# Opening of a fused recurrence and maxout kernel: larger first blocks, longer weight rows, casts after the loads, more transposes by DMA

## The chip, the cores and the metric

The kernel runs on one core of a Trainium2 chip. The core has a matrix engine (TensorE, PE), a vector engine (VectorE, DVE), a scalar engine (ScalarE, ACT), a general engine (GpSimd, POOL) and SyncE (SP), which issues DMAs. Each works through its own instructions in order and waits on semaphores for the others. The metric is the device time of one run in microseconds, lower is better.

## The reference

```python
def _attn_ref(x, f_logit, lower_bound):       # x, f_logit: 4 x 6144 x 256
    sig = 1.0 / (1.0 + np.exp(-f_logit))
    f = lower_bound + (1.0 - lower_bound) * sig
    i = 1.0 - f
    for t in range(S):
        h = f[:, t] * h + i[:, t] * x[:, t]
        y[:, t] = h
    return y

def _moe_ref(x, w1, w2, w_out):               # x = y as 24576 x 256, d_ff = 1024
    h1 = x @ w1
    h2 = x @ w2
    g = np.maximum(h1, h2)
    return g @ w_out
```

A gated recurrence runs along time, separately for each of 256 channels and 4 sequences. Its output goes through two layers: the maximum of two products, and a product with `w_out`. Inputs and output are float32.

## The kernel before

**What is computed how.** The maximum is rewritten: max(h1, h2) = h1 + relu(h2 - h1). The first layer therefore multiplies by one matrix, `wd` (w2 minus w1, scaled), and ACT takes the ReLU of it out of PSUM as `rt`. The second layer adds `rt @ wob` (`wob` is w_out in bfloat16) to `y @ w13`, where `w13` is w1 times w_out, made once in the opening. A factor of one minus the lower bound is folded into the weights (`om`).

**Blocks and chunks.** Tokens are cut into blocks of at most 512 (`TB`) and chunks of at most 1024 (`CH`). A chunk is the unit that is fetched, a block the unit that is computed. The first sequence begins with chunks of 256, 256 and 512 tokens, one block each; every other chunk has 1024 tokens and two blocks. There are 26 chunks and 49 blocks.

**Getting channels onto partitions.** The recurrence wants channels on partitions and time along the row; memory has tokens in rows of 1 KB. There are three ways (`fetch`, `cross`, `turn_steps`):

- Chunk 0 is loaded as float32 by SP, and PE transposes it.
- Other chunks that are not `by_xbar` are cast to bfloat16 in a DMA that POOL issues, into a tile `fn` or `xn`; PE transposes 128 x 128 pieces of it into PSUM (`tT`), which ACT and DVE read there.
- Chunks that are `by_xbar` are cast by a POOL DMA into a scratch buffer in device memory (six for f, six for x, used in turn), and a transposing DMA that SP issues (`cross`) brings them into `fT` or `xT`. A scratch buffer is written again only after its transposing DMA has landed. `by_xbar` holds for f from chunk 5 on, and for x from chunk 5 on except chunks 7, 11, 15, 19 and 23.

**One block.** `gate` is a sigmoid on ACT, giving `u`. `scan_steps` are five DVE steps: `drive` (u times x), two `decay` and two `scan`, giving `y`. `first_layer(j, fc)` is two matmuls of 512 columns and one ReLU; there are eight per block. `second_layer(j, slot)` is an eighth of the block's 40 matmuls of 256 columns, with two copies out of PSUM and one output DMA per block on SP.

**Order.** All instructions stand in an order written by hand (`manual_schedule`). In the opening the weights come in four column groups of 256 (rows of 1 KB); w1 is scaled on ACT (`make_w1s`), `wd` is made on DVE (`make_wd`), w1 is transposed on PE (`make_w1T`), and its product with `wob` gives `w13`. These steps are interleaved with the first three blocks. Then the loop runs over j: the first layer of block j, the second layer of block j-1, the transposes of block j+2, the scans of block j+1, and the gate of block j+2 after the middle of the block. `ahead` issues the casting DMAs 10 blocks early (`LEAD_FETCH`) and the transposing DMAs 5 blocks early (`LEAD_CROSS`). POOL does nothing but DMAs after its first instructions, so its casts run as far ahead as buffers and its queue allow, whatever the loop has reached.

Of the kernel before, what the change touches and what calls it, by code (L numbers as in the profile page):

```python
# [9 lines left out]
FP32 = mybir.dt.float32  # L10
# [8 lines left out]
def kernel(  # L19
# [71 lines left out]
    def fetch(c):  # L91
        b, t0, nt, _ = chunks[c]
        for s in range(2):
            src = srcs[s][b, t0 : t0 + nt, :]
            if c == 0:
                nat = const.tile([P, nt // P, D], FP32, name=("f0", "x0")[s])
                nc.sync.dma_start(
                    out=nat[:], in_=src.rearrange("(i p) d -> p i d", p=P)
                )
                held[c, s] = nat  # L100
            elif by_xbar(c, s):
                scr = scratch[s][uses[s] % NSCR]
                uses[s] += 1
                nc.gpsimd.dma_start(  # L104
                    out=scr[0:nt, :].rearrange("(p i) d -> p (i d)", p=P),
                    in_=src.rearrange("(p i) d -> p (i d)", p=P),
                )
# [19 lines left out]
    def turn_steps(j):  # L127
        b, t0, nb, c, o = blocks[j]
        steps = []
        for s in range(2):  # L130
            if by_xbar(c, s):
                turned[j, s] = held[c, s][:, :, o : o + nb]
                continue
            if c == 0:
                dst = ps_t.tile([P, KC, nb], FP32, name="tT")
            else:
                dst = ps_t.tile([P, KC, TB], BF16, name="tT")
            turned[j, s] = dst[:, :, 0:nb]
            for q in range(nb // P):
                for h in range(KC):  # L140
                    steps.append(
                        (
                            dst[:, h, q * P : (q + 1) * P],
                            held[c, s][:, o // P + q, h * P : (h + 1) * P],
                        )
                    )
        return steps

    def turn(steps):
        for dst, src in steps:  # L150
            nc.tensor.transpose(dst, src, ident[:] if src.dtype == BF16 else ident_f[:])  # L151

    ys = {}

# [2 lines left out]
    def gate(j):  # L157
        nb = blocks[j][2]
        u = midpool.tile([P, KC, TB], BF16, name="u")
        nc.scalar.activation(  # L160
            out=u[:, :, 0:nb], in_=turned[j, 0], func=AF.Sigmoid, scale=-1.0
        )
        us[j] = u

    def scan_steps(j):
        b, t0, nb, c, o = blocks[j]
# [14 lines left out]
            )  # L181

        def drive():
            nc.vector.tensor_tensor(  # L184
                out=v[:, :, 0:nb], in0=u[:, :, 0:nb], in1=turned[j, 1], op=ALU.mult
            )

        def scan(h):
# [22 lines left out]
    def recurrence(j):  # L211
        gate(j)
        for step in scan_steps(j):
            step()
# [1 line left out]
    ident_f = const.tile([P, P], FP32)  # L216
    make_identity(nc, ident_f[:])
    ident = const.tile([P, P], BF16)
    nc.vector.tensor_copy(out=ident[:], in_=ident_f[:])
    om = const.tile([P, KC], FP32)  # L220
    nom = const.tile([P, KC], FP32)
    lbc = const.tile([P, KC], FP32)
    warm = const.tile([P, 1], FP32)
    nc.sync.dma_start(out=lbc[:], in_=lower_bound.rearrange("(h p) -> p h", p=P))
    nc.vector.tensor_scalar(
        out=om[:], in0=lbc[:], scalar1=-1.0, scalar2=1.0, op0=ALU.mult, op1=ALU.add
    )
    nc.vector.tensor_scalar_add(out=nom[:], in0=lbc[:], scalar1=-1.0)

    w1n = wpool.tile([P, KC, DFF], FP32)  # L230
    w2n = wpool.tile([P, KC, DFF], FP32)
# [7 lines left out]
    def gcols(g):  # L239
        return slice(g * DFF // NG, (g + 1) * DFF // NG)  # L240

    def fetch_w(g):
        for w, src in ((w2n, moe_w2), (w1n, moe_w1)):
            nc.sync.dma_start(
                out=w[:, :, gcols(g)],
                in_=src[:, gcols(g)].rearrange("(kc p) f -> p kc f", p=P),
            )

    def make_w1s(g):
        for kc in range(KC):  # L250
            nc.scalar.mul(  # L251
                w1s[:, kc, gcols(g)], w1n[:, kc, gcols(g)], om[:, kc : kc + 1]
            )

    def make_wd(g):
        for kc in range(KC):
            nc.vector.scalar_tensor_tensor(  # L257
                out=wd[:, kc, gcols(g)],
                in0=w2n[:, kc, gcols(g)],
                scalar=om[:, kc : kc + 1],  # L260
                in1=w1s[:, kc, gcols(g)],
                op0=ALU.mult,
                op1=ALU.subtract,
            )

    def make_w1T(g):
        n = FC // NG
        pt = ps_o.tile([P, KC, n, P], FP32, name="psO")
        for kc in range(KC):
            for q in range(n):  # L270
                fc = n * g + q
# [3 lines left out]
        dst = w1T[:, n * g : n * g + n, :].rearrange("p q (k d) -> p k q d", k=KC)  # L275
        if g % 2:
            nc.scalar.copy(out=dst, in_=pt[:])
        else:
            nc.vector.tensor_copy(out=dst, in_=pt[:])

    def make_w13():
        for kc in range(KC):
# [84 lines left out]
    with tc.manual_schedule():  # L367
        fetch(0)
        fetch(1)
        for g in range(NG):  # L370
            fetch_w(g)
        nc.gpsimd.dma_start(
            out=wob[:], in_=moe_w_out.rearrange("(fc p) c -> p fc c", p=P)
        )
# [12 lines left out]
        turn(turn_steps(1))  # L387
        make_wd(1)
        recurrence(1)
        first_layer(0, 2)  # L390
        first_layer(0, 3)
        make_w1s(2)
        make_wd(2)
        make_w1T(0)
        make_w1T(1)
        first_layer(0, 4)
        first_layer(0, 5)
        make_w1s(3)
        make_wd(3)
        make_w1T(2)  # L400
        first_layer(0, 6)
        first_layer(0, 7)
        make_w1T(3)
        turn(turn_steps(2))
        gate(2)
        make_w13()
        done["fetch"] = 3
        ahead("fetch", fetch, LEAD_FETCH)
        ahead("cross", cross, LEAD_CROSS)
        for j in range(1, NBLK + 1):  # L410
            ahead("fetch", fetch, j + LEAD_FETCH)
            ahead("cross", cross, j + LEAD_CROSS)
            steps = turn_steps(j + 2) if j + 2 < NBLK else []
            scans = scan_steps(j + 1) if j + 1 < NBLK else []
# [40 lines left out]
```

## Time and profile before

| | |
|---|---|
| median of 3 runs | 418.28 us (418.23 to 418.82) |
| the profiled execution: time of the run | 418.23 us |
| its span, first to last instruction | 415.8 us |
| PE busy, DVE busy, ACT busy, POOL busy | 95%, 58%, 66%, 7% |
| read from device memory, written to it | 53.48 MB, 44.56 MB |
| mean granted TensorE clock | 0.992 |

Times in the profile count from the start of the span. A row of the timeline gives the start, the duration, the engine, the line of the kernel, the operation, the tile written and the tile read, and in square brackets the idle time before it and what ended that. A row of groups gives the sum of busy time and the mean duration of one in nanoseconds. A row of the windows gives the stretch, its length, the busy time of each engine, the granted clock, the busy share of the DMA engines and GB/s written. A row of DMA issues ends with the time from issue to landing. Matmuls are pipelined, so that the rate of several in a row is read from their starts.

### The profile page before, as it was taken

What the parts mean: (1) busy time and instruction counts of PE and PEld (TensorE: products, weight loads), DVE (VectorE), ACT (ScalarE), POOL (GpSimd) and SP (SyncE); (2) the same over time, 40 slices, a digit from 0 to 9 for tenths busy, and PEclk for the clock granted to TensorE, in tenths of its full rate; (3) what the DMA queues carried; (4) which work ended last, traced back from release to release, by engine and by line L of the source; (5) the groups of instructions that cost most, each with busy time, mean ns of one, the idle gap of its engine ahead of it and who ended that gap; (6) DMA issues with size and microseconds to landing.
All of it is one profiled execution on the core that took longest, in us unless ns stands there. A gap on an engine that the chain in (4) does not pass through costs nothing.

```text
span 415.8 us, 7247 instructions
## 1 busy us (share of the span) xinstructions
PE 395.5 (95%) x2872; PEld 304.8 (73%) x2920; DVE 239.3 (58%) x354; ACT 274.1 (66%) x457; POOL 30.9 (7%) x57
## 2 busy tenths in 40 slices
PE   2699997999999999999999999999999999999996
PEld 2487774777777777777777777777777777777775
DVE  2545563665665764665665566566476575566641
ACT  2667655766766766776776676676676676677662
POOL 8122001000001000010010010000000000000000
PEclk9989998999999999999999999999999999999999
DMA  8998989999799999999999999872852453811212
GB/s 192 233 232 199 223 178 230 261 240 110 135 196 217 268 249 122 237 207 173 245 251 192 184 224 251 202 177 89 192 123 82 151 112 92 203 52 50 99 54 102
DMA packets 100657, 73.09 MB, mean 176 GB/s; under 512 B 79040, under 2 KB 93888, under 8 KB 100032
## 3 DMA queue, kind: packets, MB, share of 16 engines
q1 hardware_dynamic: 87152, 46.93, 49.4%
q0 software_dynamic: 13184, 25.43, 37.6%
q8 instruction: 23, 0.38, 0.3%
q10 hardware_dynamic: 288, 0.26, 0.2%
q14 instruction: 10, 0.08, 0.1%
HBM read 53.48 MB, written 44.56 MB: 236 GB/s over the span
## 4 chain that ended last, share of the span: by engine, by line
PE 83%; DMA 15%; issue 1%; ACT 0%; POOL 0%; DVE 0%; POOLq 0%; ACTq 0%
PE psO L330 48%; PE dT L301 34%; DMA fT<-scr_0_90 7%; DMA scr_0_90<-in_f_logit_dram 6%; DMA xn<-in_x_dram 2%; PE tT L151 1%; ACT u L160 0%; POOL fn L111 0%; ACT rt L309 0%; DVE osb L339 0%; POOL ident_f masks.py:199 0%; POOL ident_f masks.py:197 0%; POOLq masks.py:199 0%; ACTq L160 0%; POOLq L439 0%
## 5 line engine op out<-in xcount | busy, mean ns | idle before, releaser
L309 ACT ACTIVATE rt<-dT 128x512 bf16<-128x512 f32 (+1 forms) x392 | 225.7, 587 | 117.8 <-PE dT L301 115.7
L330 PE MATMUL psO<-wob,rt 128*128 128x256 bf16 x1536 | 230.8, 273 | 2.3
L301 PE MATMUL dT<-y,wd 128*128 128x512 bf16 (+1 forms) x736 | 221.6, 378 | 10.1 <-DVE wd L257 7.0
L330 PEld LDWEIGHTS <-rt 128*128 128x128 bf16 x1536 | 169.6, 113 | 42.9 <-issue 0.6
L350 DVE COPY osb<-psO 128x512 f32<-128x512 f32 x94 | 65.0, 692 | 153.0 <-PE psO L330 153.0
L194 DVE TENSOR_TENSOR_SCAN y<-ff,y,v 128x512 bf16<-128x512 bf16 (+1 forms) x90 | 109.2, 1255 | 0.0
L301 PEld LDWEIGHTS <-wd 128*128 128x128 bf16 x784 | 71.9, 98 | 16.9 <-DVE wd L257 9.5
L330 PE MATMUL psO<-w_122,y 128*128 128x256 bf16 x384 | 73.7, 273 | 0.3
L330 PEld LDWEIGHTS <-y 128*128 128x128 bf16 x384 | 43.3, 113 | 41.6 <-issue 0.6
L160 ACT ACTIVATE u<-fT 128x1024 bf16<-128x1024 bf16 x42 | 44.0, 1048 | 4.0 <-DMA fT<-scr_0_90 4.0
L174 DVE TENSOR_SCALAR ff<-u,nom 128x512 bf16<-128x512 bf16 (+1 forms) x98 | 29.7, 347 | 0.0
L151 PE MATMUL tT<-ident,xn 128*128 128x128 bf16 x124 | 23.6, 228 | 0.0
L184 DVE TENSOR_TENSOR v<-u,xT 128x1024 bf16<-128x1024 bf16 x32 | 21.8, 681 | 2.2 <-DMA xT<-scr_0_96 2.2
L184 DVE TENSOR_TENSOR v<-u,tT 128x1024 bf16<-128x1024 bf16 (+1 forms) x17 | 11.3, 664 | 7.6 <-PE tT L151 4.0
L151 PEld LDWEIGHTS <-xn 128*128 128x128 bf16 x124 | 12.3, 103 | 0.3
L251 ACT ACTIVATE w1s<-w1n,om 128x256 f32<-128x256 f32 x8 | 3.6, 500 | 7.1 <-DMA w1n<-in_moe_w_dram 7.1
L194 DVE TENSOR_TENSOR_SCAN y<-ff,v 128x512 bf16<-128x512 bf16 (+1 forms) x8 | 8.3, 1074 | 0.0
L111 POOL DMA_DIRECT2D xn<-in_x_dram x9 | 7.9, 883 | 2.3 <-DMA xn<-in_x_dram 2.2
L160 ACT ACTIVATE u<-tT 128x1024 bf16<-128x1024 bf16 (+2 forms) x7 | 6.3, 898 | 2.1 <-PE tT L151 2.1
L257 DVE SCALAR_TENSOR_TENSOR wd<-w2n,om,w1s 128x256 bf16<-128x256 f32 x8 | 3.5, 479 | 4.5 <-ACT w1s L251 4.5
L151 PE MATMUL tT<-ident,fn 128*128 128x128 bf16 x44 | 6.1, 245 | 0.0
L104 POOL DMA_DIRECT2D scr_0_90<-in_f_logit_dram x4 | 2.0, 500 | 49.5 <-DMA fT<-scr_0_90 49.0
(40 smaller groups left out, 49.0 us busy)
## 6 DMA issues: line engine op xcount, KB each, us to landing
out_dram<-osb SPq DMA_DIRECT2D x46, 512.0 KB, 3.8
xn<-in_x_dram POOLq DMA_DIRECT2D x7, 512.0 KB, 15.0
scr_0_90<-in_f_logit_dram POOLq DMA_DIRECT2D x4, 512.0 KB, 9.0
scr_1_91<-in_f_logit_dram POOLq DMA_DIRECT2D x4, 512.0 KB, 7.3
scr_2_92<-in_f_logit_dram POOLq DMA_DIRECT2D x4, 512.0 KB, 14.1
scr_0_96<-in_x_dram POOLq DMA_DIRECT2D x3, 512.0 KB, 19.9
scr_1_97<-in_x_dram POOLq DMA_DIRECT2D x3, 512.0 KB, 9.9
scr_3_93<-in_f_logit_dram POOLq DMA_DIRECT2D x3, 512.0 KB, 8.6
```

The lines of the kernel that those rows point to most:

```text
L111: nc.gpsimd.dma_start(out=nat[:, 0 : nt // P, :], in_=src.rearrange("(i p) d -> p i d", p=P),)
L151: nc.tensor.transpose(dst, src, ident[:] if src.dtype == BF16 else ident_f[:])
L160: nc.scalar.activation(out=u[:, :, 0:nb], in_=turned[j, 0], func=AF.Sigmoid, scale=-1.0)
L174: nc.vector.tensor_scalar(out=ff[:, h, 0:nb], in0=u[:, h, 0:nb], scalar1=nom[:, h : h + 1], scalar2=1.0, op0=ALU.mult, op1=ALU.add,)
L184: nc.vector.tensor_tensor(out=v[:, :, 0:nb], in0=u[:, :, 0:nb], in1=turned[j, 1], op=ALU.mult)
L194: nc.vector.tensor_tensor_scan(out=y[:, h, 0:nb], data0=ff[:, h, 0:nb], data1=v[:, h, 0:nb], initial=init, op0=ALU.mult, op1=ALU.add,)
L251: nc.scalar.mul(w1s[:, kc, gcols(g)], w1n[:, kc, gcols(g)], om[:, kc : kc + 1])
L257: nc.vector.scalar_tensor_tensor(out=wd[:, kc, gcols(g)], in0=w2n[:, kc, gcols(g)], scalar=om[:, kc : kc + 1], in1=w1s[:, kc, gcols(g)], o ...
L301: nc.tensor.matmul(dT[:, 0:nb], lhsT=wd[:, kc, fc * P : (fc + 1) * P], rhs=y[:, kc, 0:nb], start=(kc == 0), stop=(kc == KC - 1),)
L309: nc.scalar.activation(out=rt[:, 0:nb], in_=dT[:, 0:nb], func=AF.Relu)
L330: nc.tensor.matmul(ps[:, r, :], lhsT=left, rhs=right, start=(s == 0 and (r == 0 or j == NBLK - 1)), stop=(s == n - 1 and (r == 1 or j == N ...
L350: nc.vector.tensor_copy(out=osb[:, 2 * g : 2 * g + 2, :], in_=ps[:])
```

## The change

- The first sequence begins with four chunks of 512 tokens (one block each) instead of 256, 256 and 512. There are 26 chunks and 48 blocks.
- Chunk 0 comes with four tokens, 4 KB, per partition and is cast to bfloat16 by DVE. The other chunks that PE transposes come with four tokens per partition as well. After the transposes the tokens of a block stand permuted in PSUM; the gate and the drive read PSUM with a stride of 128 elements to undo that (`like`).
- The weights w1 and w2 come in two column halves, rows of 2 KB; `w_out` comes in rows of 4 KB. Hidden units are permuted to suit, the same in `wd`, `w1T` and `wob`.
- POOL issues the cast of `w_out` only after the first half of w1 has landed, and all other casts only after the second half of w2 has landed (`pool_waits`).
- From chunk 6 on all of x goes by transposing DMA (`by_xbar`); chunk 5 of x is now transposed by PE.
- Transposing DMAs are issued 3 blocks early instead of 5. The gate of a block that came by transposing DMA moves from the middle of iteration j-2 to the start of iteration j-1.
- The opening finishes all eight first-layer slices of block 0 and `w13` before block 1 is turned; the loop starts at j = 2.

The core of the diff:

```diff
-        sizes = [256, 256, 512] if b == 0 else []
+        sizes = [TB] * 4 if b == 0 else []
...
-        return c >= 5 and (s == 0 or c % 4 != 3)
+        return c >= (5, 6)[s]
...
-                    out=nat[:], in_=src.rearrange("(i p) d -> p i d", p=P)
-                )
+                    out=raw[:], in_=src.rearrange("(p i) d -> p i d", p=P)
+                )
+                nat = natpool.tile([P, CH // P, D], BF16, name=("fn", "xn")[s])
+                nc.vector.tensor_copy(out=nat[:, 0 : nt // P, :], in_=raw[:])
...
-                    out=nat[:, 0 : nt // P, :],
-                    in_=src.rearrange("(i p) d -> p i d", p=P),
+                    out=nat[:, 0 : nt // P, :].rearrange(
+                        "p (k i) d -> p k (i d)", i=TB // P
+                    ),
+                    in_=src.rearrange(
+                        "(k p i) d -> p k (i d)", p=P, i=TB // P
+                    ),
...
+            turned[j, s] = dst[:, :, 0:nb].rearrange("p k (i m) -> p k m i", i=ns)
...
+        src = turned[j, 0]
         nc.scalar.activation(
-            out=u[:, :, 0:nb], in_=turned[j, 0], func=AF.Sigmoid, scale=-1.0
+            out=like(u[:, :, 0:nb], src), in_=src, func=AF.Sigmoid, scale=-1.0
         )
...
+    def like(t, src):
+        if len(src.shape) == 3:
+            return t
+        return t.rearrange("p k (m i) -> p k m i", m=P)
...
-    NG = 4
+    NG = 2
+    NQ = FC // NG
+    w1n = [wpool.tile([P, KC, NQ * P], FP32, name=f"w1n{g}") for g in range(NG)]
+    w2n = [wpool.tile([P, KC, NQ * P], FP32, name=f"w2n{g}") for g in range(NG)]
+
+    def half(w, g):
+        return w[g][:].rearrange("p kc (m q) -> p kc q m", q=NQ)
+
+    def fcs(w, kc, g):
+        return w[:, kc, g * NQ * P : (g + 1) * NQ * P].rearrange(
+            "p (q m) -> p q m", q=NQ
+        )
...
+    def pool_waits(t):
+        nc.gpsimd.tensor_copy(out=waited[:], in_=t)
...
-        if g % 2:
-            nc.scalar.copy(out=dst, in_=pt[:])
-        else:
-            nc.vector.tensor_copy(out=dst, in_=pt[:])
+        dst = w1T[:, 2 * k : 2 * k + 2, :].rearrange("p q (k d) -> p k q d", k=KC)
+        nc.scalar.copy(out=dst, in_=pt[:])
...
-    LEAD_CROSS = 5
+    LEAD_CROSS = 3
...
         fetch(0)
-        fetch(1)
         for g in range(NG):
             fetch_w(g)
-        nc.gpsimd.dma_start(
-            out=wob[:], in_=moe_w_out.rearrange("(fc p) c -> p fc c", p=P)
-        )
-        fetch(2)
...
         recurrence(0)
         make_w1s(0)
         make_w1s(1)
+        pool_waits(w1n[0][:, 0, 0:1])
+        nc.gpsimd.dma_start(
+            out=wob[:].rearrange("p (g q) c -> p g (q c)", g=NG),
+            in_=moe_w_out.rearrange("(g p q) c -> p g (q c)", g=NG, q=NQ),
+        )
+        pool_waits(w2n[1][:, 0, 0:1])
         make_wd(0)
-        first_layer(0, 0)
-        first_layer(0, 1)
-        turn(turn_steps(1))
+        for fc in range(0, NQ):
+            first_layer(0, fc)
+        fetch(1)
+        fetch(2)
+        done["fetch"] = 3
+        ahead("fetch", fetch, LEAD_FETCH)
         make_wd(1)
...
         make_w1T(0)
         make_w1T(1)
...
+        for fc in range(NQ, FC):
+            first_layer(0, fc)
         make_w1T(2)
...
         make_w1T(3)
+        make_w13()
+        turn(turn_steps(1))
+        recurrence(1)
+        for fc in range(FC):
+            second_layer(0, fc)
         turn(turn_steps(2))
-        gate(2)
-        make_w13()
-        done["fetch"] = 3
-        ahead("fetch", fetch, LEAD_FETCH)
-        ahead("cross", cross, LEAD_CROSS)
-        for j in range(1, NBLK + 1):
+        recurrence(2)
+        for fc in range(FC):
+            first_layer(1, fc)
+        turn(turn_steps(3))
+        gate(3)
+        for j in range(2, NBLK + 1):
...
+            gates = {}
+            if j + 1 < NBLK and by_xbar(blocks[j + 1][3], 0):
+                gates[0] = j + 1
+            if j + 2 < NBLK and not by_xbar(blocks[j + 2][3], 0):
+                gates[FC // 2] = j + 2
...
+                if fc in gates:
+                    gate(gates[fc])
+                if fc == 0 and j + 1 < NBLK:
+                    scans = scan_steps(j + 1)
                 if fc < len(scans):
                     scans[fc]()
-                if fc == FC // 2 and j + 2 < NBLK:
-                    gate(j + 2)
```

More of the change, by code (lines that the diff above doesn't have):

```diff
@@ L133, in turn_steps @@
                 continue
-            if c == 0:
-                dst = ps_t.tile([P, KC, nb], FP32, name="tT")
-            else:
-                dst = ps_t.tile([P, KC, TB], BF16, name="tT")
-            turned[j, s] = dst[:, :, 0:nb]
-            for q in range(nb // P):
+            dst = ps_t.tile([P, KC, TB], BF16, name="tT")
+            ns = nb // P
+            turned[j, s] = dst[:, :, 0:nb].rearrange("p k (i m) -> p k m i", i=ns)
+            for q in range(ns):
                 for h in range(KC):
@@ L150, in turn @@
         for dst, src in steps:
-            nc.tensor.transpose(dst, src, ident[:] if src.dtype == BF16 else ident_f[:])
+            nc.tensor.transpose(dst, src, ident[:])
     ys = {}
@@ L222 @@
     lbc = const.tile([P, KC], FP32)
+    waited = const.tile([P, 1], FP32)
     warm = const.tile([P, 1], FP32)
-    nc.sync.dma_start(out=lbc[:], in_=lower_bound.rearrange("(h p) -> p h", p=P))
-    nc.vector.tensor_scalar(
-        out=om[:], in0=lbc[:], scalar1=-1.0, scalar2=1.0, op0=ALU.mult, op1=ALU.add
-    )
-    nc.vector.tensor_scalar_add(out=nom[:], in0=lbc[:], scalar1=-1.0)
-    w1n = wpool.tile([P, KC, DFF], FP32)
-    w2n = wpool.tile([P, KC, DFF], FP32)
     wob = wpool.tile([P, FC, D], BF16)
@@ L250, in make_w1s @@
         for kc in range(KC):
[L251 to L253 removed]
+            nc.scalar.mul(fcs(w1s, kc, g), half(w1n, g)[:, kc], om[:, kc : kc + 1])
+    def pool_waits(t):
+        nc.gpsimd.tensor_copy(out=waited[:], in_=t)
     def make_wd(g):
@@ L257, in make_wd @@
             nc.vector.scalar_tensor_tensor(
-                out=wd[:, kc, gcols(g)],
-                in0=w2n[:, kc, gcols(g)],
+                out=fcs(wd, kc, g),
+                in0=half(w2n, g)[:, kc],
                 scalar=om[:, kc : kc + 1],
-                in1=w1s[:, kc, gcols(g)],
+                in1=fcs(w1s, kc, g),
                 op0=ALU.mult,
@@ L264, in make_wd, with make_w1T @@
             )
-    def make_w1T(g):
-        n = FC // NG
-        pt = ps_o.tile([P, KC, n, P], FP32, name="psO")
+    def make_w1T(k):
+        pt = ps_o.tile([P, KC, 2, P], FP32, name="psO")
         for kc in range(KC):
-            for q in range(n):
-                fc = n * g + q
+            for q in range(2):
+                fc = 2 * k + q
                 nc.tensor.transpose(
```

37 lines of the change are left out of this document (15 added, 22 removed).

## The prediction

> **What bounds the kernel now.** I read the page's first and fourth parts, then the chain in order of time, then the timeline of the opening and of the one hole, then the groups by form, then the DMA answers.
>
> ```profile
> span 415.8 us, 7247 instructions
> PE 395.5 (95%) x2872; PEld 304.8 (73%) x2920; DVE 239.3 (58%) x354; ACT 274.1 (66%) x457; POOL 30.9 (7%) x57
> 139.75 0.71 PE psO L330 x5
> 147.57 0.71 PE psO L330 x5
> 155.44 0.71 PE psO L330 x5
> 163.71 0.71 PE psO L330 x5
> 171.92 0.71 PE psO L330 x5
> 179.74 0.71 PE psO L330 x5
> 37.41 0.15 PEld L301 LDWEIGHTS <-wd 128*128 128x128 bf16 x2
> 407.69 0.22 PEld L330 LDWEIGHTS <-y 128*128 128x128 bf16 x2
> ```
>
> The span is 415.8 us and the profiled run took 418.23, so 2.4 us lie outside the span; the median of the runs is 418.28, practically the same. TensorE (PE) is busy 95% of it. The five-matmul pieces come once per block of 512 tokens: 7.82 us apart (139.75 to 147.57; 171.92 to 179.74) where PE only multiplies. Around 155 to 172 the three steps sum to 24.35 instead of 23.46: there PE also turned the x of one 1024-token chunk, 16 transposes, 0.89 us, or 0.056 each. From 37.41, where the third whole block's iteration starts (j=3), to 407.69, where only the last second layer is left, are 370.28 us for 46 iterations. At 7.82 that is 359.7; 10.6 us are extra. The other losses are the opening (37.4 us) and a tail of 8.1 us that the change leaves alone. The extra has a hole in it:
>
> ```profile
> 62.61 0.10 PEld L301 LDWEIGHTS <-wd 128*128 128x128 bf16 x1
> 64.12 1.06 ACT L160 ACTIVATE u<-fT 128x1024 bf16<-128x1024 bf16 x1 [4.02 <-DMA fT<-scr_0_90]
> 65.71 1.01 PE L301 MATMUL dT<-y,wd 128*128 128x512 bf16 x2 [2.83 <-ACT rt L309]
> 65.00:68.50 3.50, 2.79 (x10) 1.34 (x10) 1.22 (x3) 2.23 (x5) 0.94 (x2) 0.51 1.57 386
> ```
>
> ScalarE (ACT) waited 4.02 us for the first chunk turned by DMA, its ReLUs stood behind that wait, PE starved for 2.83 us, and then ran 3.5 us at a granted clock of 0.51, which is another 1.7. Together 4.4 to 4.5 us. Transposes make up the rest of the 10.6: 112 after 37.41, 6.2 us.
>
> **The change, part by part.** *Transposes in the loop.* From the point equal to 37.41 (in the new kernel the start of j=2, since its blocks 0 and 1 cover the old 0 to 2) 48 are left: f and x of chunk 4, x of chunk 5. 48 x 0.056 = 2.7 us against 6.2: **3.5 us gained**, on PE's path, as PE never waits there. What replaces them are four more DMA transposes, weighed below.
>
> *The opening.* The rows that price it:
>
> ```profile
> 10.05 0.91 ACT L251 ACTIVATE w1s<-w1n,om 128x256 f32<-128x256 f32 x2 [4.18 <-DMA w1n<-in_moe_w_dram]
> 13.18 0.91 ACT L251 ACTIVATE w1s<-w1n,om 128x256 f32<-128x256 f32 x2 [2.23 <-DMA w1n<-in_moe_w_dram]
> 4.00:5.00 1.00, 1.00 (x8) 0.83 (x6) 0.00 (x0) 0.00 (x0) 1.00 (x3) 1.00 1.20 265
> 20.00:25.00 5.00, 4.45 (x33) 3.98 (x34) 1.87 (x4) 2.63 (x5) 0.97 (x2) 0.66 1.45 198
> 22.30 1.06 PE L151 MATMUL tT<-ident,fn 128*128 128x128 bf16 x8
> 23.46 1.02 ACT L160 ACTIVATE u<-tT 128x1024 bf16<-128x1024 bf16 x1 [0.32 <-PE tT L151]
> 24.01 1.97 PE L285 MATMUL psO<-wob,w1T 128*128 128x256 bf16 x16
> 25.11 0.61 DVE L174 TENSOR_SCALAR ff<-u,nom 128x512 bf16<-128x512 bf16 x2
> 25.64 2.45 DVE L194 TENSOR_TENSOR_SCAN y<-ff,y,v 128x512 bf16<-128x512 bf16 x2
> L309 ACT ACTIVATE rt<-dT 128x512 bf16<-128x512 f32 x376 | 220.0, 596 | 115.0 <-PE dT L301 113.0 <-PE psO L330 1.5
> L257 DVE SCALAR_TENSOR_TENSOR wd<-w2n,om,w1s 128x256 bf16<-128x256 f32 x8 | 3.5, 479 | 4.5 <-ACT w1s L251 4.5
> L184 DVE TENSOR_TENSOR v<-u,tT 128x1024 bf16<-128x1024 bf16 x15 | 10.2, 678 | 3.1 <-ACT u L160 3.1
> L279 DVE CAST w1T<-psO 128x512 bf16<-128x512 f32 x2 | 1.4, 684 | 0.0
> 407.41 4.93 PE psO L330 x45
> ```
>
> Without casts beside it SP's queue gets six tiles of 512 KB: f0, x0, and two halves of each of w2 and w1. No row shows that queue alone. Below, it got 512 KB in 3.13 us beside casts (10.05 to 13.18, 168 GB/s); above, casts alone wrote 198 GB/s, which is 396 read. Nearest is the second from 4.0, mostly this queue: 265 written and, with casts read at twice their size, about 310 read. I take 310: 1.7 us a tile from 2.4 us (f0's first packets), 0.4 for the landing: f0 4.5, x0 6.2, w1's first half 9.6, its second 13.4 with some of w_out beside it.
>
> The casts of f0 and x0 are new on VectorE (DVE): 1024 elements, above 1.37 (twice the 684 ns of 512 from PSUM), below 0.61 (two decays, 1024 elements of bf16 from SBUF); I take 0.8, nearer the second, as it reads no PSUM. The drive now reads PSUM with a stride: between 0.68 as it stands and 1.37; I take 1.37. The sigmoid I leave at 1.02, for ACT takes elements one at a time in every row; were the stride to double it, each of three blocks in the opening would pay 1 us. Then y of block 0 is at 6.2 + 0.8 + 1.06 + 1.37 + 0.61 + 2.45 = 12.5, and two wd pieces of 512 (0.75 each, between one and two of 479) make 14.0. But ACT holds w1s of the second half (2 x 0.75, from 13.4) ahead of block 0's ReLUs: 14.9. From there ACT is the chain: 8 ReLUs of 0.59 and 4 copies of w1's transposes of 0.59 (two of these came from DVE) end at 22.0; the last 10 of w13's 16 matmuls (1.97 for all) 23.2; 16 transposes 1.8; second layer of block 0, 40 matmuls at 0.11 (45 in 4.93), 29.4; meanwhile gate, drive, decays and scans give y of block 1 at 29.6. 16 transposes, 31.2; the next 8 ReLUs pace the first layer, PE done 34.7; 16 transposes, 36.5. These transposes are at the half clock of that row (0.66 mean from 20 to 25); at 0.056 each the same sum gives 35.0. I take 36.0 for the start of j=2, **1.4 us earlier** than 37.41. PE there has done the same matmuls, so nothing is owed later. POOL's two waits delay only casts: the chunk 1 that block 1 needs at 23 is queued from about 11 behind w_out, 2 MB read at 396 GB/s, 17. The wait costs nothing there; its cost would be at the far end of the casts.
>
> *The hole.* Its price depends on those casts:
>
> ```profile
> 38.70 0.51 POOL L104 DMA_DIRECT2D scr_5_95<-in_f_logit_dram  x1 [2.10 <-DMA scr_1_91<-in_f_logit_dram]
> 41.29 0.49 POOL L104 DMA_DIRECT2D scr_4_100<-in_x_dram  x1 [2.08 <-DMA scr_1_97<-in_x_dram]
> scr_4_100<-in_x_dram POOLq DMA_DIRECT2D x1, 512.0 KB, 21.8
> fT<-scr_0_90 SPq DMA_TRANSPOSE x1, 30.7
> q0 software_dynamic: 128, 2.10, 97.7%
> q1 hardware_dynamic: 129, 0.03, 2.0%
> ```
>
> Casts run ahead without pause until their six scratch buffers are full, one 1024-token tile each 2.6 us; the last landed at 41.29 + 21.8 = 63.1. The transposing DMA issued at 33.33 took 30.7 us, to 64.0: it all but stood still until the casts were over. The last two rows (50 to 60 us) say why: both queues moved the same number of packets, the casts' 16 KB each on average, the others 0.2 KB. In the new kernel the casts queue w_out (2.6), six half tiles (7.8) and 14 whole ones up to chunk 10 (37.1) from about 10.7, plus 1.2 beside w1 and 2.6 for two outputs: over at 62.0. The first fT, now issued only after block 1's output at about 45, then lands near 63.3. Its gate is now at the start of j=5: 36.0 + 3 x 7.82 + 2.2 of transposes = 61.7. With three PSUM buffers PE can go on to the fifth slice, 61.7 + 4 x 1.03 = 65.8; the gate is over at 64.4 and the next ReLU at 65.0. **The hole closes, 4.4 us**, by under 1 us.
>
> *Where a rule speaks against it.* The Trainium skill, "DMA: Bandwidth & Descriptors", section "Issuing engines are not separate DMA queues", says that all queues share 16 engines, so moving work between them saves only issue time. By it holding casts back moves bytes and gains no bandwidth, and the run would be the 413 of rival one below. The trace agrees as far as it goes: with both queues at work the second from 4.0 moved 265 GB/s, and no row shows SP's queue alone. Before the end of the casts both kernels read the same: 19.4 MB by casts and 2.6 by SP before, 18.9 and 3.1 after.
>
> *Lead.* Each DMA transpose is issued 3 blocks ahead instead of 5, and the gate of a DMA-turned block moves from the middle of j-2 to the start of j-1. Time from issue to need shrinks from 3.5 blocks (27.4 us) to 2 (15.6), plus about 3 us before PE starves. That the gate comes later in the block costs nothing by itself: DVE's first scan stands behind the copy at 59.01 below, which itself waited 2.21 us for PE's fourth slice, 3.9 us into a block, and one ReLU, gate, drive and decays (0.6 + 1.05 + 0.68 + 0.61) are over by then.
>
> ```profile
> 59.01 0.69 DVE L350 COPY osb<-psO 128x512 f32<-128x512 f32 x1 [2.21 <-PE psO L330]
> 88.64 3.72 SPq L122 DMA_TRANSPOSE fT<-scr_3_93  x1
> 181.38 11.06 SPq L122 DMA_TRANSPOSE fT<-scr_3_93  x1
> fT<-scr_3_93 SPq DMA_TRANSPOSE x1, 22.6
> fT<-scr_5_95 SPq DMA_TRANSPOSE x1, 4.9
> xT<-scr_1_97 SPq DMA_TRANSPOSE x1, 4.5
> ```
>
> Alone (near 306 us) a pair takes 5 us each; beside casts up to 22.6. I expect 10 to 14, inside 15.6 + 3: no cost.
>
> **Sum.** 36.0 + 359.7 + 2.7 + 8.1 = 406.5 us of span, 408.9 of run: **409.0**. Against 418.3 that is 1.4 from the opening, 3.5 from transposes, 4.4 from the hole.
>
> **Rivals.** *One: the hole stays.* If the same 22.0 MB go at the old mean rate (2.4 to 63.1) and two whole outputs beside them instead of a half one add 1.9 us, casts end at 65.0, fT lands at 66.2, the next ReLU is at 67.9, 2.1 after PE runs dry; the half clock adds 1.7: 412.7, and the old 4.4 whole gives 413.4. I say 413. For it: equal bytes; against: casts alone have the better rate. *Two: the loads don't get faster alone.* At 168 GB/s six tiles end at 21.4 instead of 13.4, all later steps shift by 8: 417. Against it: 265 GB/s in the second from 4.0. *Three, the slower side: the DMA side becomes the loop's clock.* fT's are issued six chunks apart at 88.64 and 181.38, 15.46 us a chunk, with only five xT among them, against PE's 15.64. One more xT, at some 10 us of SP's time, makes 17.1. With 13 chunks cast from then on and 3 us of slack, 13 x 1.5 - 3 = 16: 425. It decides from a chunk cycle of 16.6 on. For it: 22.6 us once already, with the lead cut; against: most of these cycles carried a backlog from the late start, and the lone pair needs 5 of 15.6 us.
>
> **How the numbers follow.** Forecast 0.62 (its own range 406 to 411), rival one 0.22 (411 to 415), two 0.07, three 0.09. The range 406 to 416 leaves out two and three. Under 0.2% (0.8 us), about what a measurement can tell, counts as the same: of rival two 0.05 is same, 0.02 faster. Faster 0.86, same 0.05, slower 0.09.
>
> **What would show it.** Transposes: PE instructions of the turning line fall by 64, and only j=2 to 5 are longer than 7.82. Opening: first-layer iteration j=2 starts at 35 to 36.5, with ACT's ReLUs back to back behind w1's second half at 13 to 14. Hole: the gate of block 6 waits under 3 us and the granted clock stays at 1. Lead: no wait of ACT or DVE for fT or xT later. I am wrong if casts end past 64, if w1's second half lands past 16, or if waits for fT recur each chunk.

## The result and the profile after

| | before | changed |
|---|---|---|
| median, 4 runs each | 418.55 us (418.23 to 419.21) | 408.36 us (408.01 to 408.65) |
| profiled execution: time, span | 418.23, 415.8 us | 408.01, 405.9 us |
| mean granted TensorE clock | 0.992 | 1.0 |

The ratio is 0.9754, with a 95% interval of 0.9737 to 0.9771. 409.0 was forecast. Here and below, medians count every run, and ratios leave out those that took over 1.5% longer than the fastest of the same kernel. The page of the changed kernel: its first line, the busy rows of its first part, the clock row of the second, and one row of the groups.

```profile
span 405.9 us, 7061 instructions
...
PE 388.1 (96%) x2792; PEld 297.3 (73%) x2840; DVE 247.2 (61%) x345; ACT 273.4 (67%) x446; POOL 28.0 (7%) x59
...
PEclk9999999999999999999999999999999999999999
...
L195 DVE TENSOR_TENSOR v<-u,tT 128x1024 bf16<-128x1024 bf16 x8 | 9.7, 1218 | 16.2 <-ACT u L165 14.9
```

Before, the clock row had two slices below 9; now there is none. PE has 80 matmuls fewer: 64 transposes (48 of f and 64 of x are left of 176), and 16 because the first 1024 tokens are two blocks and not three.

Now the timeline of the changed kernel: the opening, the start of j=2 (33.78), the gate of block 6 with what followed (63.63 and 65.22), and the last second layer (397.69).

```profile
4.74 0.69 DVE L101 CAST fn<-f_128 128x1024 bf16<-128x1024 f32 x1 [1.59 <-DMA f_128<-in_f_logit_dram]
9.99 2.29 ACT L266 ACTIVATE w1s<-w1n_118,om 128x512 f32<-128x512 f32 x2 [2.41 <-DMA w1n_118<-in_moe_w_dram]
12.66 2.31 ACT L266 ACTIVATE w1s<-w1n_119,om 128x512 f32<-128x512 f32 x2 [0.38 <-DMA w1n_119<-in_moe_w_dram]
...
14.88 1.26 ACT L321 ACTIVATE rt<-dT 128x512 bf16<-128x512 f32 x2
20.79 2.41 PE L297 MATMUL psO<-wob,w1T 128*128 128x256 bf16 x16
23.03 0.61 PE L155 MATMUL tT<-ident,fn 128*128 128x128 bf16 x8
29.91 4.02 ACT L321 ACTIVATE rt<-dT 128x512 bf16<-128x512 f32 x8
33.78 0.15 PEld L313 LDWEIGHTS <-wd 128*128 128x128 bf16 x2
...
63.63 1.06 ACT L165 ACTIVATE u<-fT 128x1024 bf16<-128x1024 bf16 x1 [2.65 <-DMA fT<-scr_0_90]
65.22 0.59 PE L313 MATMUL dT<-y,wd 128*128 128x512 bf16 x2 [1.24 <-ACT rt L321]
...
397.69 0.22 PEld L342 LDWEIGHTS <-y 128*128 128x128 bf16 x2
```

Where the 9.9 us of span came from, by the same three stretches as before the change:

| | before | changed | gained |
|---|---|---|---|
| start of the 46 iterations | 37.41 | 33.78 | 3.6 |
| transposes within them | 6.2 | 2.8 | 3.4 |
| hole at the first chunk turned by DMA | 4.4 | 1.4 | 3.0 |
| tail after the last second layer starts | 8.1 | 8.2 | -0.1 |

The 46 iterations took 397.69 - 33.78 = 363.91 us; at the 7.82 that a plain block takes they would take 359.7. The 4.2 over are the iterations j=2 to j=5, which still carry transposes (1.06, 0.89, 0.45 and 0.45 us), and the rest of the hole: PE stood 1.24 us (65.22) and the iteration was 1.4 longer. At full clock, the second part of the old hole is gone.

The DMA answer for 35 to 50 us of the changed kernel (each row: transfer, queue, kind, count, size, us from issue to landing):

```profile
scr_4_100<-in_x_dram POOLq DMA_DIRECT2D x1, 512.0 KB, 21.1
out_dram<-osb SPq DMA_DIRECT2D x1, 512.0 KB, 18.1
fT<-scr_0_90 SPq DMA_TRANSPOSE x1, 19.6
```

The last of the casts that run ahead was issued at 40.81 and landed at 40.81 + 21.1 = 61.9. The first transposing DMA was issued at 43.97 and landed at 63.5, 1.6 us after the casts were over, so it stood still beside them as before.

### The profile page after: what moved, and what is told of

The parts are those of the page before. It is cut to its first block, busy times and chain, and to the rows that moved or that the text cites. A ratio compares the mean times of both kernels' runs of the same rounds, so it can differ in the third digit from the quotient of the medians.

```text
span 405.9 us, 7061 instructions
## 1 busy us (share of the span) xinstructions
PE 388.1 (96%) x2792; PEld 297.3 (73%) x2840; DVE 247.2 (61%) x345; ACT 273.4 (67%) x446; POOL 28.0 (7%) x59
## 4 chain that ended last, share of the span: by engine, by line
PE 82%; DMA 14%; issue 1%; SPq 0%; POOL 0%; ACT 0%; DVE 0%; ACTq 0%
PE psO L342 49%; PE dT L313 34%; DMA fT<-scr_0_90 5%; DMA scr_0_90<-in_f_logit_dram 4%; DMA scr_4_94<-in_f_logit_dram 3%; DMA w1n_118<-in_moe_w_dram 2%; DMA fn<-in_f_logit_dram 1%; POOL waited L269 0%; SPq L97 0%; ACT rt L321 0%; POOL wob L398 0%; SPq L380 0%; SPq L259 0%; DVE osb L351 0%; PE tT L155 0%
## 5 line engine op out<-in xcount | busy, mean ns | idle before, releaser
L321 ACT ACTIVATE rt<-dT 128x512 bf16<-128x512 f32 x384 | 223.3, 598 | 109.5 <-PE dT L313 93.4
L313 PE MATMUL dT<-y,wd 128*128 128x512 bf16 x720 | 218.5, 382 | 6.9 <-DVE wd L273 5.6
L208 DVE TENSOR_TENSOR_SCAN y<-ff,y,v 128x512 bf16<-128x512 bf16 x88 | 107.8, 1266 | 0.0
L195 DVE TENSOR_TENSOR v<-u,xT 128x1024 bf16<-128x1024 bf16 x40 | 27.7, 692 | 55.0 <-ACT u L165 55.0
L184 DVE TENSOR_SCALAR ff<-u,nom 128x512 bf16<-128x512 bf16 x96 | 29.3, 347 | 0.0
L195 DVE TENSOR_TENSOR v<-u,tT 128x1024 bf16<-128x1024 bf16 x8 | 9.7, 1218 | 16.2 <-ACT u L165 14.9
L165 ACT ACTIVATE u<-tT 128x1024 bf16<-128x1024 bf16 x6 | 6.2, 1039 | 7.6 <-PE tT L155 7.5
L208 DVE TENSOR_TENSOR_SCAN y<-ff,v 128x512 bf16<-128x512 bf16 x8 | 9.3, 1206 | 0.0
L155 PE MATMUL tT<-ident,xn 128*128 128x128 bf16 x64 | 8.6, 230 | 0.3 <-DVE xn L101 0.3
L155 PEld LDWEIGHTS <-xn 128*128 128x128 bf16 x64 | 5.4, 103 | 0.6 <-DVE xn L101 0.6
```

Of the source, the lines that this page charges most:

```text
L155: nc.tensor.transpose(dst, src, ident[:])
L165: nc.scalar.activation(out=like(u[:, :, 0:nb], src), in_=src, func=AF.Sigmoid, scale=-1.0)
L184: nc.vector.tensor_scalar(out=ff[:, h, 0:nb], in0=u[:, h, 0:nb], scalar1=nom[:, h : h + 1], scalar2=1.0, op0=ALU.mult, op1=ALU.add,)
L195: nc.vector.tensor_tensor(out=like(v[:, :, 0:nb], src), in0=like(u[:, :, 0:nb], src), in1=src, op=ALU.mult,)
L208: nc.vector.tensor_tensor_scan(out=y[:, h, 0:nb], data0=ff[:, h, 0:nb], data1=v[:, h, 0:nb], initial=init, op0=ALU.mult, op1=ALU.add,)
L313: nc.tensor.matmul(dT[:, 0:nb], lhsT=wd[:, kc, fc * P : (fc + 1) * P], rhs=y[:, kc, 0:nb], start=(kc == 0), stop=(kc == KC - 1),)
```

## The experiments

Twelve runs of ten kernels (three were run a second time, the changed kernel among them) were made in three groups, each group on one chip beside the kernel before, whose medians there were 419.64, 419.96 and 419.38 us. Edits are to the changed kernel unless said otherwise. Theory: the gain is three separate terms (earlier loads through the held casts, fewer transposes, the hole closed by the later gate), and the shorter lead is free. Rivals: the held casts move bytes and gain nothing; the lead is itself a gain; the 2 KB rows make the loads fast.

### The held casts

```diff
-        pool_waits(w1n[0][:, 0, 0:1])
         nc.gpsimd.dma_start(
...
-        pool_waits(w2n[1][:, 0, 0:1])
```

> The changed kernel without POOL's two waits; everything else as changed. My theory: beside casts SP's queue gets 512 KB per 3.1 us as in the kernel before, so w1's second half lands near 21 instead of 12.6, block 0's ReLUs start 8 us later, iteration j=2 starts near 42 instead of 33.8, and the hole of 1.4 us at the first fT closes since PE is later: 415 us. The rival, the page's rule that all queues share the same engines and order gains nothing: within 1 us of 408.4.

418.2 us (417.51 to 418.86), ratio 0.9964 (0.995 to 0.9978): nearly the whole gain is gone. Its timeline:

```profile
16.18 2.29 ACT L266 ACTIVATE w1s<-w1n,om 128x512 f32<-128x512 f32 x2 [8.54 <-DMA w1n<-in_moe_w_dram]
23.69 2.30 ACT L266 ACTIVATE w1s<-w1n,om 128x512 f32<-128x512 f32 x2 [5.22 <-DMA w1n<-in_moe_w_dram]
...
46.00 0.15 PEld L313 LDWEIGHTS <-wd 128*128 128x128 bf16 x2
```

The halves of w1 came at 16.2 and 23.7 in place of 10.0 and 12.7, and j=2 started 12.2 us later. Some 8 us had been expected; part of the surplus is PE at a granted clock of 0.5 for 6.8 us from 25.4 on, after it had stood still waiting for weights. The casts, started from 1.3, were over by about 59, and the hole was not there, which gives 1.4 back. The bytes are the same in both kernels. What the wait changes is which of them are served first, and that is worth 8.8 us by the ratios, (0.9964 - 0.9754) x 418.6, and 9.8 by the medians.

The same wait alone in the kernel before, ahead of its POOL DMAs:

```diff
+        nc.gpsimd.tensor_copy(out=waited[:], in_=w2n[:, 0, gcols(2)][:, 0:1])
+        fetch(1)
```

> The kernel before with one thing of the change: POOL issues casts only after the third group of w2 has landed. My theory: weights land by about 11 instead of 19.3 and the loop starts 3 to 5 us earlier, but its gate of block 7 still waits for an fT that lands only when the casts end (63 or later), so what the opening gains the hole takes back: 417 to 420 us. The rival, that the opening's gain is kept: 414 to 415.

421.6 us (419.98 to 422.68), ratio 1.0059 (1.0035 to 1.0082): slower than before, which neither theory nor rival gave. Its timeline in the opening, at the start of j=3 and at the hole:

```profile
14.16 0.61 PE L151 MATMUL tT<-ident,fn 128*128 128x128 bf16 x4 [4.05 <-DMA fn<-in_f_logit_dram]
...
28.92 0.28 PE L151 MATMUL tT<-ident,xn 128*128 128x128 bf16 x2 [0.88 <-DMA xn<-in_x_dram]
...
37.38 0.15 PEld L302 LDWEIGHTS <-wd 128*128 128x128 bf16 x2
...
66.95 1.06 ACT L160 ACTIVATE u<-fT 128x1024 bf16<-128x1024 bf16 x1 [6.90 <-DMA fT<-scr]
68.55 1.01 PE L302 MATMUL dT<-y,wd 128*128 128x512 bf16 x2 [5.71 <-ACT rt L310]
```

w1's last group landed at 12.82 and not at 19.33, yet j=3 began at 37.38, as before (37.41). In this opening chunk 1 is now the late one: its casts stood behind the wait too, and PE waited 4.05 us for its f (14.16), with ACT's later pieces of w1s behind that block's gate. Of the earlier weights 1.1 us were left at block 1's first layer (24.63, where the kernel before had 25.71), and most of that went at 28.92, where PE waited 0.88 us for the x of chunk 3. The casts meanwhile ended 2.9 us later (65.98), and the hole grew: ACT waited 6.90 and not 4.02. So the wait alone does not pay where the first block has 256 tokens and the next chunk is held back as well, and it shifts the price to the far end of the casts, where something has to absorb it. That the larger first blocks are what makes it pay in the changed kernel is argued from these rows; no run changed the blocks alone.

### The gate and the transposes

```diff
             gates = {}
-            if j + 1 < NBLK and by_xbar(blocks[j + 1][3], 0):
-                gates[0] = j + 1
-            if j + 2 < NBLK and not by_xbar(blocks[j + 2][3], 0):
+            if j + 2 < NBLK:
                 gates[FC // 2] = j + 2
```

> The changed kernel with the gate of every block at its old place, in the middle of iteration j-2. My theory: the gate of block 6 then stands on ACT from about 55.5 while its fT lands at 63.5 as before, so PE runs dry near 60 instead of 64 and the hole is about 5 us plus the half clock's 1.7: 413 to 414 us. The rival (the place of the gate is indifferent, casts and loads made the gain): 408.4.

414.9 us (413.76 to 415.35), ratio 0.9884 (0.986 to 0.9908). Its timeline at the gate of block 6, and its windows answer for the stretch behind it:

```profile
63.68 1.06 ACT L165 ACTIVATE u<-fT 128x1024 bf16<-128x1024 bf16 x1 [5.80 <-DMA fT<-scr]
65.27 1.01 PE L313 MATMUL dT<-y,wd 128*128 128x512 bf16 x2 [4.38 <-ACT rt L321]
```

```profile
64.00:70.80 6.80, 5.53 (x22) 3.06 (x22) 1.75 (x3) 3.75 (x7) 0.96 (x2) 0.50 1.28 261
```

fT landed at the same moment, 63.6, but the gate stood 5.80 us in front of the ReLUs, PE starved for 4.38 and then ran at a granted clock of 0.50. The later gate is worth about 6 us here (the profiled spans differ by 6.9, of which 1.0 is j=2 beginning at 34.81), more than the 4.4 of the old hole, since the loop now arrives earlier.

```diff
     def by_xbar(c, s):
-        return c >= (5, 6)[s]
+        return c >= 5 and (s == 0 or c % 4 != 3)
```

> The changed kernel with the old choice of what goes by transposing DMA (x of chunk 5 does, x of chunks 7, 11, 15, 19, 23 is turned by PE): 64 more PE transposes. My theory: 64 x 0.056 = 3.6 us more, and 1 to 3 us of a larger hole as two transposing DMAs wait for the end of the casts: 413 us. The rival, that PE's transposes hide under other limits: 408.4 to 409.

414.18 us (412.6 to 414.64), ratio 0.9864 (0.9837 to 0.9891). Five chunks of x are turned by PE again and chunk 5's is not: four times 0.89 is 3.6 us. The other 2, by the medians, are a larger hole:

```profile
64.64 1.06 ACT L165 ACTIVATE u<-fT 128x1024 bf16<-128x1024 bf16 x1 [3.74 <-DMA fT<-scr]
66.23 1.01 PE L313 MATMUL dT<-y,wd 128*128 128x512 bf16 x2 [2.55 <-ACT rt L321]
66.59 0.69 DVE L195 TENSOR_TENSOR v<-u,xT 128x1024 bf16<-128x1024 bf16 x1 [6.09 <-DMA xT<-scr]
```

Chunk 5's x is here a transposing DMA too, behind the same casts, and the drive waited 6.09 us for it. Leaving the x of chunk 5 to PE, 0.89 us of work, is therefore a part of what closes the hole.

### The rows, and a better kernel

```diff
-            nc.sync.dma_start(
-                out=w[g][:],
-                in_=src[:, cols].rearrange("(kc p) f -> p kc f", p=P),
-            )
+            for h in range(2):
+                part = slice(h * NQ * P // 2, (h + 1) * NQ * P // 2)
+                nc.sync.dma_start(
+                    out=w[g][:, :, part],
+                    in_=src[:, cols][:, part].rearrange("(kc p) f -> p kc f", p=P),
+                )
```

> The changed kernel with each of the four weight loads cut into two of 256 columns, so rows of 1 KB as before, with the casts still held back. My theory: held-back casts, not row length, made the loads fast, so w1's second half lands within 0.5 us of 12.6 and the time stays within 0.6 us of 408.4. The rival: rows of 1 KB move at the 310 GB/s of the old opening's second from 4.0 against 390 now, 1.4 us later on ACT's chain, part of it taken from the hole: 409 to 410.

406.98 us (406.47 to 408.0), ratio 0.9702 (0.9679 to 0.9726). The landing came out as expected (w1's second half at 12.72, against 12.64), the time did not: it is 1.4 below. So the same kernel ran once more, with the changed kernel beside it.

> Weight rows of 1 KB once more, now beside the changed kernel. If its 406.98 is real, it is 1 to 2 us under the changed kernel here; my theory says where from: the hole of 1.4 us at the first fT is absent. The rival, that rows of 1 or 2 KB make no difference: within 0.5 us of it.

> The changed kernel itself, beside the others. The ratio to the kernel before should be 0.975 again (0.974 to 0.978) if the wide spread of e5, e7 and e9 comes from those kernels; if the chip alone was restless, the changed kernel should spread as widely on some chip too.

406.8 us (406.51 to 407.52) against 408.31 (five runs within 407.57 to 408.72, a sixth at 415.05): ratios to the kernel before of 0.9702 (0.9669 to 0.9735) and 0.9729 (0.9692 to 0.9767). These intervals overlap; the runs beside each other do not, by a narrow margin (the slowest of the one took 407.52, the fastest of the other 407.57). First the timeline of the kernel with the split loads, then that of the changed kernel:

```profile
9.66 0.18 POOL L271 COPY waited<-w1n 128x1 f32<-128x1 f32 x1 [8.35 <-DMA w1n<-in_moe_w_dram]
9.78 0.86 POOL L400 DMA_DIRECT2D wob<-in_moe_w_out_dram  x1
...
62.78 1.06 ACT L165 ACTIVATE u<-fT 128x1024 bf16<-128x1024 bf16 x1 [1.46 <-DMA fT<-scr]
```

```profile
10.15 0.86 POOL L269 COPY waited<-w1n 128x1 f32<-128x1 f32 x1 [8.84 <-DMA w1n<-in_moe_w_dram]
10.94 0.86 POOL L398 DMA_DIRECT2D wob<-in_moe_w_out_dram  x1
...
64.10 1.06 ACT L165 ACTIVATE u<-fT 128x1024 bf16<-128x1024 bf16 x1 [3.06 <-DMA fT<-scr]
65.69 0.59 PE L313 MATMUL dT<-y,wd 128*128 128x512 bf16 x2 [1.64 <-ACT rt L321]
```

POOL waits for the first column of a half. With two loads per half the first of them releases it: w_out was issued at 9.78 and not at 10.94 (0.5 of that is the earlier release, the rest POOL's copy, 0.18 us in place of 0.86), the casts ended at 61.10 and not at 62.36, and fT came 1.3 earlier. The gate then waited 1.46, which PE's buffers cover, and the 1.64 of idle PE went; j=2 began 0.3 later. The rows of 2 KB bring no more than 0.6 us on the loads. By these runs the kernel with the split loads is some 1.4 us faster than the changed one. The edit shortens the rows and splits the wait at once; that the gain comes from the wait is read from the rows above, no run has the one without the other.

### Keeping the casts off the first transposing DMA

Here the casts stop, by a third wait, until the first transposing DMA has landed:

```diff
         ahead("fetch", fetch, LEAD_FETCH)
+        ahead("cross", cross, 6)
+        pool_waits(held[5, 0][:, 0, 0:1])
```

> The changed kernel with the first transposing DMA (f of chunk 5) issued in the opening and a third POOL wait: casts from chunk 8 on only after it has landed. My theory: it lands when the casts up to chunk 7 are over, near 46 to 47, so the gate of block 6 waits for nothing, the 1.4 us hole closes and no other opens: 407.0 us. The rival: the casts that are held back come later and push the next fT past its need (75.7), so that a new hole takes the place of the old: 408.4 or more.

425.65 us (422.4 to 434.39), ratio 1.0116 (1.0073 to 1.0159): slower than the kernel before. The first fT did land at 46.56 and block 6 waited for nothing. The price came afterwards. The waits of this kernel (who waits for which transfer: total us, times, longest), and then its DMA issues:

```profile
DVE v L195 <- DMA xT<-scr: 46.5, 11, 6.5
ACT u L165 <- DMA fT<-scr: 24.4, 13, 4.3
```

```profile
fT<-scr SPq DMA_TRANSPOSE x21, 14.9
xT<-scr SPq DMA_TRANSPOSE x20, 9.1
```

The postponed casts ran until 73.4, the second fT took 16.5 us beside them, and every later one, until the casts gave out near 317 us, met casts and took 13.5 to 18.4 us, about as long as PE's whole cycle of 15.64 for a chunk, so that fT or xT was late for chunk after chunk. This is rival three of the prediction, brought about by the edit. A variant, run twice, also gives every second copy of w1's transposes to DVE:

```diff
-        nc.scalar.copy(out=dst, in_=pt[:])
+        (nc.vector.tensor_copy if k % 2 else nc.scalar.copy)(out=dst, in_=pt[:])
```

> The kernel of e5 with two of the four copies of w1's transposes given back to DVE, which sits idle then. My theory: ACT's chain in the opening shortens by up to 1.07 us, of which PE's own chain lets through about 0.5: 406.5 us. The rival: w13 waits for PE and not for ACT, no change against e5.

> The kernel of e9 (casts from chunk 8 on held back for the first fT, two copies on DVE) beside the changed kernel. My theory after e5's trace: holding casts back puts the DMA queues a chunk behind, each transposing DMA then runs beside the casts of the chunk before, a chunk takes 15 to 19 us of DMA against PE's 15.64, and PE waits here and there: 415 to 430, most runs. The rival, that e5 and e9 met a restless chip: 405.5 to 407 and clearly under the changed kernel.

The first time (median 427.2 us) the profiled run took 407.07 us, with a median fT of 10.7 us and no wait for fT above 0.9, and the other five 423.5 to 433.7. The second time (median 419.56) two of six took 406.24 and 408.73, the others 418.85 to 427.44. So the twelve runs of one program fall in two groups, 10 us and more apart. One of each kind was profiled; what decides between them from run to run stays open. The copies gained nothing: j=2 began at 34.53 and 33.81.

Another way is to cut the casts into small packets, by writing the scratch in runs of 512 bytes:

```diff
-                    out=scr[0:nt, :].rearrange("(p i) d -> p (i d)", p=P),
-                    in_=src.rearrange("(p i) d -> p (i d)", p=P),
+                    out=scr[0:nt, :].rearrange("(i p) d -> p i d", p=P),
+                    in_=src.rearrange("(i p) d -> p i d", p=P),
```

> The changed kernel with the casts into scratch cut into runs of 512 B instead of 4 KB and more. My theory (packets of the two queues are served in turn, so large cast packets starve the 256 B packets of a transposing DMA): the first fT, issued at 44, lands near 52 to 56 instead of 63.5, the hole closes, 407 us if casts keep their rate. The rival, that the first fT waits for casts by bandwidth and not by packet size: it lands at 63 or later and the time is 408.4 or more; if small runs slow the casts, more.

413.12 us (411.55 to 419.67), ratio 0.9831 (0.9797 to 0.9865). Its DMA answers for 35 to 50 us, for 50 to 60 (queue: packets, MB, share of 16 engines), and a later row of its timeline:

```profile
fT<-scr SPq DMA_TRANSPOSE x1, 15.2
```

```profile
q0 software_dynamic: 2191, 1.11, 79.8%
q1 hardware_dynamic: 2191, 0.95, 51.3%
```

```profile
82.56 0.69 DVE L195 TENSOR_TENSOR v<-u,xT 128x1024 bf16<-128x1024 bf16 x1 [4.77 <-DMA xT<-scr]
```

The first fT landed at 60.30 while casts went on until 72.6; in the changed kernel it landed only when they were over. Again both queues moved the same number of packets, but now 0.95 MB of them were SP's in 10 us (an output of 0.5 MB among them), where it was 0.03 MB before the change; both queues together moved about the same, 2.06 and 2.13 MB. So what starves a transposing DMA is the size of the packets it takes turns with. It also missed its aim: the casts paid, the last one taking 30.7 us and not 21, and x came late at 82.56.

### The lead

```diff
-    LEAD_CROSS = 3
+    LEAD_CROSS = 5
```

> The changed kernel with transposing DMAs issued 5 blocks ahead again. My theory: the first fT is issued near 32 instead of 44 but stands still until the casts end, landing near 63; later ones had time to spare: within 0.5 us of 408.4. The rival, that the shorter lead made a gain by itself (less mixing of casts and transposing DMAs): 410 or more.

419.14 us (twelve runs, 413.38 to 424.82), ratio 0.9944 (0.9907 to 0.9981): the theory's "free" was wrong, the rival right. The shorter lead is worth 8 us by the ratios, 10.8 by the medians. The waits and DMA issues with a lead of five (the profiled run took 423.63 us, near the upper end), and the DMA issues of the changed kernel:

```profile
DVE v L195 <- DMA xT<-scr: 35.4, 8, 6.8
...
ACT u L165 <- DMA fT<-scr: 20.6, 9, 4.7
```

```profile
fT<-scr SPq DMA_TRANSPOSE x21, 15.3
xT<-scr SPq DMA_TRANSPOSE x20, 8.9
```

```profile
fT<-scr SPq DMA_TRANSPOSE x21, 5.4
xT<-scr SPq DMA_TRANSPOSE x20, 4.5
```

Why three times as long? One chunk cycle of each, first with a lead of five:

```profile
190.03 0.49 POOL L106 DMA_DIRECT2D scr<-in_f_logit_dram  x1 [16.09 <-DMA fT<-scr]
190.78 9.18 SPq L128 DMA_TRANSPOSE fT<-scr  x1
191.68 0.62 POOL L106 DMA_DIRECT2D scr<-in_x_dram  x1 [1.17 <-DMA xT<-scr]
```

and the changed kernel:

```profile
188.48 2.64 SPq L128 DMA_TRANSPOSE fT<-scr  x1
...
194.20 0.49 POOL L106 DMA_DIRECT2D scr<-in_f_logit_dram  x1 [13.08 <-DMA fT<-scr]
196.07 0.49 POOL L106 DMA_DIRECT2D scr<-in_x_dram  x1 [1.39 <-DMA xT<-scr]
...
204.12 2.53 SPq L128 DMA_TRANSPOSE fT<-scr  x1
```

A landed transposing DMA frees a scratch buffer, and POOL at once casts into it. With a lead of three SP issues the next fT 8 us after those casts (204.12 behind 196.07), when the f cast has landed (200.66) and the x cast nearly has (205.15): transposes and casts take turns. With a lead of five the next fT is issued 0.75 us behind the f cast that the last one released (190.78), runs beside it, lands late, releases the next cast late, and so meets that one too. That the lead costs this time is shown by the run; the loop is read from the rows.

Undone one at a time, the wait, the gate, the choice of transposes and the lead cost 9.8, 6.5, 5.8 and 10.8 us by the medians, 33 in all, where the whole change gained 10.2. So they are not separate terms, as the theory had it: each is worth that much only with the others in place.

## Why the prediction was right, and where it was not

**Transposes in the loop:** 3.5 predicted, 3.4 measured. PE never waited there, so instructions times duration was enough.

**The opening:** 1.4 predicted, 3.6 measured, the mis-sized term. The path was the right one, and its first two thirds came within 0.3 us: ReLUs from 14.88 (14.9 predicted), ACT's chain to 21.87 (22.0), w13 to 23.2 (23.2). Within that, errors offset each other, which is luck: w1's second half landed earlier (12.64, not 13.4), the pieces of w1s and wd were slower (1.15 and 1.06, not 0.75). The error lies behind 23.2, and j=2 missed its sign of 35 to 36.5. I took the three sets of 16 transposes at 1.6 to 1.8 us each, from the half clock of the old opening, which gave 36.5; the granted clock was 1.00 from 20 to 34 us, and each set took 0.9 (the first from 23.03 to 23.92). My sum for the full clock, 35.0, was a slip in adding: the same chain with 0.9 off each of three sets gives 36.5 - 2.7 = 33.8, which is what was measured. Its other two steps were close: the second layer of block 0 took 4.4 (23.92 to 28.29; 4.4 taken), the first layer of block 1 3.8 (29.18 to 32.94; 3.5 taken). One profile fixes this term to about 1 us only: in those of the runs above with the same opening (the gate's old place, the old choice of transposes, the lead of five, the changed kernel again) j=2 began between 33.84 and 34.81. The strided drive took 1.22, nearer to the 1.37 chosen than to the other bound.

**The casts and the hole:** casts over at 62.0 predicted, 61.9 measured; fT landed at 63.3 predicted, 63.5 measured. The hole was to close, 4.4 us, and gave 3.0. That is the opening's error coming back: j=5 started at 59.63 and not at 61.7, and so met the same landing 2.1 us earlier, when the margin was "under 1 us". The run without the wait shows it from the other side: there j=2 came 12.2 us later, and the hole was not there. What is gained ahead of a fixed landing is paid there in part; the two terms should have been written as one. Their sum, 5.8 predicted and 6.6 measured, is why the total held.

**The lead:** "no cost" came true, but not for the reason given. I expected 10 to 14 us a transposing DMA inside a slack of 15.6 + 3. The first ones after the start come near that (the second took 11.0), and then the time falls to 5 or 6. The step looked only at time from issue to need; by it the old lead would have cost nothing either, and with it the run took 419.14 us. So this term of the sum was right by luck. It missed that the issue time decides what runs beside the transfer, and that the landing of one releases the casts that disturb the next. The casts kept off the first transposing DMA and the lead of five both tip that loop.

**Rivals.** *One,* 413, had its ground in the Trainium skill, "DMA: Bandwidth & Descriptors", section "Issuing engines are not separate DMA queues": all queues share the same engines, so that spreading DMAs over issuing engines saves only issue time; that order gains nothing was drawn from it, the section does not speak of order. As to bandwidth the runs agree: the wait gained none, and with it the casts were over later, at 61.9 and not at 59.1. As to time the inference doesn't hold: the bytes that PE needed first were there at 12.64 and not at 23.67, and the run was 8.8 to 9.8 us shorter. *Two,* slow loads, is out: the six tiles, 3.15 MB, came from 2.4 to 12.64, 307 GB/s in the mean, where 310 was taken and 168 feared. The pace was not even: 410 GB/s from 8 to 10 us, 263 from 6 to 8; why it dipped stays open. *Three,* the DMA side as the clock, did not occur in the changed kernel's profile, but is near: one lead or one wait away. Whether the changed kernel's one run at 415.05 was such a run has no trace to say.

Not tried: the larger first blocks or their 4 KB rows by themselves, and the split loads together with other edits.

## What to carry to other kernels

Order a shared DMA system by need: hold bulk transfers behind the few loads that the first work waits for, release the hold with the smallest load that will do, and then look at the far end of the bulk transfers, where the delay turns up again. Issue a transfer of small packets late enough to run alone, above all where its landing releases large ones; a longer lead can make it later. When summing a path, don't price instructions at a clock of the stretch that the change removes, add the chain again for every value that is tried in it, and write a gain and the fixed event that it runs into as one term.

## What the runs showed of the hardware

- Two DMA queues at work took turns by packet: equal counts in 10 us whether one's packets were 16 KB (128 and 129) or 0.5 KB (2191 each). Near the end of the casts the counts part (111 and 172 in the changed kernel from 50 to 60). A transposing DMA of 512 KB took 4.5 to 5.4 us in the median of the changed kernel, 12 to 19 (fT) beside one chunk's casts with a lead of five, and 14 to 31 beside the casts that run ahead.
- SP's queue with nothing beside it read weight rows of 2 KB at 406 GB/s from 8 to 9 us (397 in the second profile of the changed kernel), rows of 1 KB at 383 and 372 in the two profiles with split loads.
- Reading PSUM with a stride cost DVE 1.22 against 0.68 us for 1024 elements; it cost ACT's sigmoid nothing (1.02 us either way).
- Doubling a w1s piece to 512 elements, read with a stride of four elements, took it from 0.46 to 1.15 us, more than twice.
